# Rings as single buffers taken in turn, tiles taken by their first writer, and a new written-out order, in a fused linear attention and channel-mix kernel

## The chip, the cores and the metric

The kernel runs on one core of a Trainium2 chip. Its time is device microseconds of one launch. The profile's span is the stretch in which the profiler saw work on the core.

## The reference

Two layers follow each other. The first is linear attention with a learned feature map (8 batches, 8 heads, 576 positions, head size 64, 128 features):

```
phi(x) = concat(exp(p), exp(-p)),  p = x @ w_phi - max|x @ w_phi|
kv  = einsum('bhsf,bhsd->bhfd', phi(k), v);   z = sum over s of phi(k)
out = (phi(q) @ kv) / (phi(q) . z + 1e-6)
```

The heads are then laid side by side (x: 8 x 576 x 512), and the second layer mixes channels:

```
x_prev = x shifted by one position (zero ahead)
xk = mu_k*x + (1-mu_k)*x_prev;   xr = mu_r*x + (1-mu_r)*x_prev
k  = max(xk @ w_k, 0)            # 512 -> 1024
v  = (k*k) @ w_v                 # 1024 -> 512
out = sigmoid(xr @ w_r) * v
```

Inputs and output are float32; matmuls run on bfloat16.

## The kernel before

**Units of work.** Attention goes by pairs of heads, numbered n = 4b + a (batch b from 0 to 7, pair a from 0 to 3), so 32 pairs. The channel mix goes by batch b, in blocks of 512 positions, and once per two batches for the 64 positions that are left over of each ("edge"). Every step of a unit has a short name, and these names are used throughout:

- Loads of batch b: `lk`, `lq` (k and q, issued by POOL's software queue, L321, into tile nat), `lv` (v, issued by SP or POOL, L327, into vt). For batches 2 to 7, `tr b.0` and `tr b.2` (L352) transpose the first and second half of nat into qkT by DMA, issued by SP. For batches 0 and 1, PE does it (`pt`, L338), and `pa`, `pb` copy the result. The first batches' loads are split finer (`lk0.1`, `lk0.2`). `wk`, `wr`, `wv` load the weights.
- Pair n: `kp`, `qp` project k and q on PE (L566); `rk`, `rq` take the maximum of |.| on DVE (L579, L584); `em` (ACT, L591), `mh` (DVE or POOL), `mt` (PE) and `mc` (DVE or ACT) prepare the scale; `ea` is the exponential of k on ACT (L605); `va`, `vb` multiply v by the scale, on POOL or DVE (L597); `qt` projects q again, transposed (L630, L636); `qa`, `qb` are its exponentials on ACT (L643; `eb` is the second exponential of k); `kv` (L656, L662) is the product of phi(k) and v, `kc` its copy; `nd` (L677) gives numerator and denominator, `ra` the reciprocal (DVE, L685), `rd` the division into x_sc (DVE, L689).
- Pair n, then: x has to be transposed into xs. Below n = 8 PE does it (`xt`, L715, with copies `xe`, `xf`); from n = 8 on SP issues a DMA transpose (`xz`, L700) and `xu` does two small copies. `df` is the difference of neighbouring positions (L726), `xa` and `xb` the two mixes (DVE, L732).
- Edge of attention, per batch: the left-over rows of all pairs go through `tp` (PE, L466), `rt`, `mhe`, `mte`, `mce`, `eme`, `ekt`, `qte`, `eqe`.
- Channel mix of batch b: `h b.0` to `h b.7` (PE, L810), `rl` (relu, ACT L206 or DVE L208), `sq` (square, ACT L212, or DVE or POOL L214), `r b.0` to `r b.3` (PE, L829), `th` (tanh form of the sigmoid, ACT, L835), `v b.0` to `v b.3` (PE, L843, eight matmuls each), `ob` (DVE, L849) and `so` (the store, two DMAs on SP, L856). Edges `he`, `rle`, `sqe`, `re`, `the`, `ve`, `obe`, `soe` are the same for the left-over positions.

**What sets the order.** The string ORDER at the head of the file lists all steps, and Plan.order() turns it into the list in which they are emitted. Scheduling by the framework is off. Each engine, and SP as a queue, runs its own steps strictly in the order of this list; waits between engines come from which tiles a step reads and writes. In a word such as `kp5:0`, the number behind the colon is the PSUM place; `/POOL` names the engine where there is a choice; `+2@1` adds two filler matmuls. Words that end in `.d` mark where a DMA's end stood in the list and emit nothing.

**Buffers.** A tile in SBUF is asked for from a pool with a number of buffers, `bufs`, and the pool gives out one that is free. BUFS lists the numbers: nat 2, qkT 2, vt 3, k and q exponentials 2 each, kk 2, krelu 3, rt 3, ob 4, x 3, d (diff) 2 and so on. The tile of a relu (krelu) is asked for in `h`, ahead of the matmuls that fill PSUM, that of a gate (rt) in `r`, and that of an output (ob) in `v`:

```
s["kr", fc] = mm.tile([128, 512], BF, name="krelu", bufs=BUFS["krelu"])   # in h
s["t", ci] = mm.tile([128, DM], BF, name="rt", bufs=BUFS["rt"])           # in r
s["o", ci] = mm.tile([128, DM], FP, name="ob", bufs=BUFS["ob"])           # in v
```

Work overlaps across batches: while the channel mix of batch b runs on PE, the attention of batch b + 1 and the loads of batch b + 2 and later go on.

Of the kernel before, what the change touches and what calls it, by code (L numbers as in the profile page):

```python
# [31 lines left out]
eb3 pt6.1:0 pt7.0:1 va2/POOL pb6/DVE tr6 qt2:2 pa7/ACT ra1 rd1 mte0.2:0 qa2 lk2.0 lk2.0.d pt7.1:1
mce0.2/DVE qp5:0 pb7/DVE tr7 qte0.2:0 lq2.0 lq2.0.d qb2 rq5 tp1.0:1 xt0:1 va3/POOL eqe0.2 kv2:2
rt1.0 xf0/ACT xe0/ACT kp4:0 mh4/POOL mt3:0 kc2/ACT rk4 xt1:1 df0/POOL mc3/ACT ekt1.0 nd2:2 ra2 ea4
vb3/POOL xe1/DVE qt3:1+1@0 rd2 mt4:0 xf1/ACT mc4/ACT df1/DVE qa3 xt2:1 xa0 kv3:2 eb4 mhe1.0/DVE
xe2/DVE mte1.0:0+1@0 xb0 kc3/ACT kp5:0 qb3 qt4:2 xa1 eme1.0 xf2/DVE nd3:1 rk5 mce1.0/ACT df2/POOL
qa4 ra3 qb4 rd3 lv1.2/POOL lv1.2.d ea5 xa2 xt3:0+7@1 qp6:2 xb1 qte1.0:1 xe3/ACT qp7:1 eb5 xf3/DVE
df3/DVE xa3 em4 qt5:0+1@0 eqe1.0 rq6 vb4/POOL h0.0:0 qa5 va4/POOL rq7 kp6:2 qb5 h0.1:1 rk6 mh6/POOL
kp7:1 rl0.1/ACT kv4:0 va5/POOL rl0.0/ACT tr2.0 tr2.0.d tr8 tr9 mt6:1 kc4/DVE ea6 h0.2:0 rk7 vb5/POOL
eb6 xb2 kv5:0+1@2 mc6/ACT sq0.0/ACT xb3 nd4:2 tr2.2 tr2.2.d tr10 tr11 em6 ea7 h0.3:1 kc5/DVE  # L40
vb6/POOL ra4 rd4 nd5:0 eb7 vb7/POOL rl0.3/DVE qt6:2 rl0.2/ACT ra5 qp8:1 rd5 qa6 lv2.0/SP lv2.0.d
sq0.1/POOL r0.0:1 rq8 qb6 va6/POOL qp9:0 h0.4:0 rq9 th0.0 sq0.3/POOL sq0.2/ACT qt7:2 kv6:1 rl0.4/DVE
qa7 lk3.0 lk3.0.d tp2.0:0 kc6/DVE h0.5:1 mh8/POOL rt2.0 qb7 va7/POOL xt4:0 rl0.5/ACT kp8:1 xf4/DVE
# [12 lines left out]
eqe3.0 r1.0:1 rq12 em12 r1.1:0 th1.0 va12/POOL ea13 so0.0 so0.0.d rq13 qp14:1 h1.2:1 vb12/POOL eb13
xz10 xz10.d rq14 nd11:2 rl1.2/ACT va13/POOL qp15:0 th1.1 ra11 lv3.2/SP lv3.2.d h1.3:1 rd11 xu8/ACT
xu9/POOL sq1.1/ACT so0.3 so0.3.d mh12/POOL rq15 kv12:1 sq1.2/ACT vb13/POOL kp14:2 kc12/ACT h1.4:0
rk14 rl1.3/ACT mh14/POOL sq1.3/POOL mt12:1 kv13:1 mc12/ACT so0.1 so0.1.d rl1.4/DVE ea14 kp15:0
# [101 lines left out]
def kernel(  # L161
# [141 lines left out]
    def get(dct, key, pool, shape, dtype, name, **kw):  # L303
        if key not in dct:
            dct[key] = pool.tile(shape, dtype, name=name, **kw)
# [711 lines left out]
```

## Time and profile before

| | |
|---|---|
| time, median of 3 runs | 277.98 us (277.68 to 287.12) |
| span of the profiled execution | 275.3 us (no other time of that execution is given) |
| granted TensorE clock | 1.00 in each window of 10 us |
| PE, DVE, ACT, POOL busy | 261.7, 234.6, 223.1, 142.4 us |
| read from and written to HBM | 33.62 and 9.44 MB |
| instructions | 8865 |

The page gives the busy time of each engine, then the span in 40 slices of 6.9 us (a digit is the busy share in tenths), the DMA queues, the chain of work that ended last, the costliest groups of instructions (operation, tiles, shape, number | busy time, mean ns of one | idle time ahead of them and what ended it), and the DMA issues with the time to landing. "SPq" is SP's queue of issues. Matmuls of PE are pipelined, and their ends are modelled, so a busy PE isn't one at its peak.

### The profile page before, as it was taken

Reading aid. Unit: us, or ns where it says so; the run is one execution under the profiler, and the core shown is the slowest. Engines: PE = TensorE matmul, PEld = TensorE weight load, DVE = VectorE, ACT = ScalarE, POOL = GpSimd, SP = SyncE. Lnnn points to the kernel's source line nnn. Section 1 sums busy time; section 2 is a strip of 40 time slices with the busy share of each in tenths; the row PEclk is TensorE's granted clock in tenths of the full one; section 3 lists DMA queues with packets and bytes.
Section 4 is the critical chain, followed back from the end, with each engine's and each line's share of the span. In section 5 each row is a group of like instructions: output and inputs, shape, how many; then the busy total and the mean of one; then the engine's idle time right before and its main releaser. Section 6 shows DMA issues by size and latency. Waiting matters only on the chain.

```text
span 275.3 us, 8865 instructions
## 1 busy us (share of the span) xinstructions
PE 261.7 (95%) x3682; PEld 154.1 (56%) x3730; DVE 234.6 (85%) x388; ACT 223.1 (81%) x413; POOL 142.4 (52%) x193
## 2 busy tenths in 40 slices
PE   7899889999899999999999999999999999999993
PEld 3567656566555566555565666555566565444542
DVE  6999999999799989999999889998889897864222
ACT  3899999999899997899898999789987777616330
POOL 5799557976818682633459465821931611300200
PEclk9999999999999999999999999999999999999999
DMA  7999999599999899759699998981725324142134
GB/s 147 285 209 250 209 213 174 114 235 175 238 129 200 202 219 185 155 127 248 99 166 164 215 249 142 171 255 41 161 89 88 77 52 100 42 110 67 29 88 116
DMA packets 65817, 42.89 MB, mean 156 GB/s; under 512 B 47152, under 2 KB 57008, under 8 KB 65776
## 3 DMA queue, kind: packets, MB, share of 16 engines
q1 hardware_dynamic: 54496, 27.54, 49.3%
q0 software_dynamic: 11056, 14.42, 29.1%
q8 instruction: 29, 0.48, 0.8%
q10 hardware_dynamic: 224, 0.36, 0.5%
q14 instruction: 12, 0.10, 0.1%
HBM read 33.62 MB, written 9.44 MB: 156 GB/s over the span
## 4 chain that ended last, share of the span: by engine, by line
PE 75%; DVE 8%; ACT 6%; issue 4%; DMA 3%; POOL 2%; SPq 0%; POOLq 0%; ACTq 0%
PE ps_h L810 19%; PE ps_v L843 17%; PE ps_r L829 9%; PE ps_nd L677 5%; PE ps_kv L656 5%; DMA qkT<-nat 3%; PE ps_he L897 3%; PE ps_ve L929 3%; PE ps_k L566 2%; PE ps_qT L630 2%; PE ps_q L566 2%; PE ps_qT L636 2%; ACT k L605 2%; DVE nmk L579 2%; PE ps_f L292 1%
## 5 line engine op out<-in xcount | busy, mean ns | idle before, releaser
L597 POOL TENSOR_TENSOR v<-vt,v 128x576 bf16<-128x576 f32 x59 | 69.8, 1203 | 33.5 <-ACT v L591 31.1
L605 ACT ACTIVATE k<-ps_k 128x1024 bf16<-128x1024 f32 x64 | 64.8, 1047 | 1.3 <-DVE nmk L579 1.3
L643 ACT ACTIVATE q<-ps_qT 128x1024 bf16<-128x1024 f32 x64 | 63.8, 1054 | 1.8 <-PE ps_qT L636 1.7
L810 PE MATMUL ps_h<-xk,wk_bf 128*128 128x512 bf16 x235 | 60.5, 380 | 1.2
L843 PE MATMUL ps_v<-wv_bf,kk 128*128 128x512 bf16 x244 | 58.2, 379 | 0.6
L579 DVE TENSOR_REDUCE nmk<-ps_k 128x8 f32<-128x1024 f32 x32 | 38.8, 1217 | 1.8 <-PE ps_k L566 1.5
L584 DVE TENSOR_REDUCE nmq<-ps_q 128x8 f32<-128x1024 f32 x32 | 38.3, 1217 | 1.6 <-PE ps_q L566 1.4
L843 PEld LDWEIGHTS <-kk 128*128 128x128 bf16 x256 | 24.1, 98 | 27.3
L810 PEld LDWEIGHTS <-wk_bf 128*128 128x128 bf16 x256 | 22.7, 97 | 25.0 <-issue 0.7
L206 ACT ACTIVATE krelu<-ps_h 128x512 bf16<-128x512 f32 x48 | 28.8, 611 | 9.3 <-PE ps_h L810 9.3
L726 POOL TENSOR_TENSOR diff<-xs 128x576 bf16<-128x576 bf16 x15 | 20.2, 1346 | 28.8 <-ACT xs L706 12.7
L214 POOL TENSOR_TENSOR kk<-krelu 128x512 bf16<-128x512 bf16 x18 | 19.1, 1068 | 30.3 <-ACT krelu L206 26.6
L849 DVE SCALAR_TENSOR_TENSOR ob<-rt,ps_v 128x512 f32<-128x512 bf16 x32 | 21.7, 682 | 14.3 <-PE ps_v L843 12.7
L829 PE MATMUL ps_r<-wr_bf,xr 128*128 128x512 bf16 x116 | 31.1, 380 | 0.7
L835 ACT ACTIVATE rt<-ps_r 128x512 bf16<-128x512 f32 x32 | 19.7, 615 | 8.8 <-PE ps_r L829 8.7
L732 DVE SCALAR_TENSOR_TENSOR xk<-diff,mu_k_t,xs 128x576 bf16<-128x576 bf16 x32 | 26.7, 839 | 0.1
L689 DVE TENSOR_TENSOR x_sc<-ps_nd,rden 128x640 bf16<-128x640 f32 x32 | 26.0, 817 | 0.6
L732 DVE SCALAR_TENSOR_TENSOR xr<-diff,mu_r_t,xs 128x576 bf16<-128x576 bf16 x32 | 25.6, 806 | 0.1
L656 PE MATMUL ps_kv<-v,k 64*128 64x65 bf16 x1024 | 22.4, 190 | 0.5 <-ACT q L643 0.2
L566 PEld LDWEIGHTS <-qkT 64*128 64x128 bf16 x512 | 16.5, 94 | 11.0 <-issue 8.0
L656 PEld LDWEIGHTS <-k 64*128 64x128 bf16 x1024 | 19.3, 94 | 5.7 <-issue 1.8
L677 PE MATMUL ps_nd<-kv,q 128*128 128x65 bf16 x512 | 21.4, 193 | 0.0
(102 smaller groups left out, 414.3 us busy)
## 6 DMA issues: line engine op xcount, KB each, us to landing
out_dram<-ob SPq DMA_DIRECT2D x70, 128.0 KB, 2.5
vt<-in_v_dram SPq DMA_DIRECT2D x11, 576.0 KB, 6.1
nat<-in_k_dram POOLq DMA_DIRECT2D x6, 576.0 KB, 7.8
nat<-in_q_dram POOLq DMA_DIRECT2D x6, 576.0 KB, 8.0
vt<-in_v_dram POOLq DMA_DIRECT2D x4, 576.0 KB, 6.0
wk_bf<-in_moe_w_k_dram POOLq DMA_DIRECT2D x2, 512.0 KB, 11.4
wv_bf<-in_moe_w_v_dram POOLq DMA_DIRECT2D x2, 512.0 KB, 10.6
nat<-in_k_dram POOLq DMA_DIRECT2D x3, 288.0 KB, 6.9
```

Source lines behind the costliest of these rows:

```text
L206: nc.scalar.activation(out_, in_, AF.Relu, scale=HALF)
L579: nc.vector.tensor_reduce(t[:, j, :], s["k"].rearrange("p a (g f) -> p (a g) f", f=128), axis=AX.X, op=ALU.max, apply_absolute_value=True, ...
L584: nc.vector.tensor_reduce(t[:, j, :], s["q"].rearrange("p a (g f) -> p (a g) f", f=128), axis=AX.X, op=ALU.max, apply_absolute_value=True, ...
L597: (nc.vector if eng == "DVE" else nc.gpsimd).tensor_tensor(vb[:, a, pn, :, 0:64], vt[b, a // 2][:, a % 2, :].rearrange("p (s d) -> p s d", ...
L605: nc.scalar.activation(s[f"k{pn}"], s["k"].rearrange("p a (g f) -> p (a g) f", f=128), AF.Exp, scale=(1.0 if pn == 0 else -1.0))
L643: nc.scalar.activation(t.rearrange("f x (a p) -> f x a p", a=2), s["qT"].rearrange("f a (x p) -> f x a p", p=64), AF.Exp, scale=(1.0 if pn ...
L656: nc.tensor.matmul(ps[:, hh, pn * 65:(pn + 1) * 65], lhsT=s[f"k{pn}"][r, c, :], rhs=vb[r, a, pn, 2 * g + par, :], start=(pn == 0 and c == ...
L677: nc.tensor.matmul(ps[:, bk, o * 65:(o + 1) * 65], lhsT=tail if sl < 2 else s[f"q{pn}"][:, 2 * G + h, :], rhs=s["kv"][:, h, pn, :], start= ...
L732: nc.vector.scalar_tensor_tensor(out=t[:, a, (b % 2) * S:(b % 2 + 1) * S], in0=s["d"], scalar=mu[:, a:a + 1], in1=xs[:, a, 0:S], op0=ALU.m ...
L810: nc.tensor.matmul(ps, lhsT=wk_bf[:, c, fc * 128:(fc + 1) * 128], rhs=xkt[bp][:, c, m0:m0 + 512], start=(c == 0), stop=(c == NDC - 1))
L829: nc.tensor.matmul(ps, lhsT=xrt[bp][:, c, m0 + ci * 128:m0 + (ci + 1) * 128], rhs=wr_bf[:, c, :], start=(c == 0), stop=(c == NDC - 1))
L843: nc.tensor.matmul(ps, lhsT=s["kk"][:, fc, ci * 128:(ci + 1) * 128], rhs=wv_bf[:, fc, :], start=(fc == 0), stop=(fc == NFC - 1))
```

## The change

Three things change, and nothing that is computed.

1. Every ring of buffers becomes a set of tiles with one buffer each, named by their place (`krelu.0`, `krelu.1`, ...), which are taken in turn by a counter. BUFS gets entries for rden (3, what the pool gave it before) and kke (1).
2. The tiles krelu, rt and ob are asked for by the step that first writes them (`rl`, `th`, `ob`) and no longer by the matmuls ahead of it.
3. ORDER is written anew: the same steps with other places in the list, and for some another engine (the square `sq`, the relu `rl`, the small copies `mc`, `xu`, `kc`, the difference `df`, a v multiply and the v loads). PSUM places change with it. The diff shows only two stretches of the list, where batches 4 and 5 are fetched.

```diff
+    used = {}
+
+    def slot(kind):
+        i = used[kind] = used.get(kind, -1) + 1
+        return i % BUFS[kind]
+
+    def ring(pool, kind, shape, dtype, name, i=None):
+
+        i = slot(kind) if i is None else i
+        return pool.tile(shape, dtype, name=name, tag=f"{name}.{i}", bufs=1)
+
     nat, qkT, vt = {}, {}, {}
 
-    def get(dct, key, pool, shape, dtype, name, **kw):
+    def get(dct, key, pool, kind, shape, dtype, name):
         if key not in dct:
-            dct[key] = pool.tile(shape, dtype, name=name, **kw)
+            dct[key] = ring(pool, kind, shape, dtype, name)
         return dct[key]
...
-                s["kr", fc] = mm.tile([128, 512], BF, name="krelu", bufs=BUFS["krelu"])
                 if fc == 0:
-                    s["kk"] = mm.tile([128, NFC, 512], BF, name="kk")
+                    s["kk"] = ring(mm, "kk", [128, NFC, 512], BF, "kk")
...
         def rl(fc):
             def f(eng):
+                s["kr", fc] = ring(mm, "krelu", [128, 512], BF, "krelu")
                 relu(eng, s["kr", fc], s[fc])
             return f
...
             def f():
+                s["t", ci] = ring(mm, "rt", [128, DM], BF, "rt")
                 nc.scalar.activation(s["t", ci], s["r", ci], AF.Tanh, scale=0.5)
...
             def f():
+                s["o", ci] = ring(mm, "ob", [128, DM], FP, "ob")
                 nc.vector.scalar_tensor_tensor(out=s["o", ci], in0=s["t", ci], scalar=1.0,
...
-mce3.0/DVE ob0.3 tr4.0 tr4.0.d tr16 tr17 h1.0:0 qa11 xb6 h1.1:1 qb11 ra10 xb7 kv11:2 rl1.0/ACT rd10
-kp13:0 eme3.0 tr4.2 tr4.2.d tr18 tr19 sq1.0/POOL qte3.0:0 kc11/DVE rl1.1/ACT qp12:1 rk13 qp13:2
...
-ra14 rd13 df11/POOL qb15 rd14 re0:1 xu12/POOL so1.1 so1.1.d sqe0.1/DVE ob1.2 kp17:2 the0 kv15:0 rk17
-xz13 xz13.d qt16:1 kc15/ACT v1.3:1 xb11 ea17 tr5.2 tr5.2.d tr22 tr23 sqe0.0/DVE eb17 xa10 nd15:0
...
+r1.0:1 rk13 r1.1:0 xz8 tr4.2 so0.2 xz9 lv3.2/SP xz10 so0.1 tr4.0 xz8.d sq1.0/ACT lv3.0.d xz9.d th1.0
...
+xz11.d xu11/DVE ra13 rd13 df11/POOL tr5.0 xz12 so1.1 lv4.0/SP so1.0 xz13 tr5.2 xz13.d xz12.d so0.2.d
...
```

The order of SP's queue around these places, before: ... so0.2, xz8, xz9, tr4.0, tr4.2, so0.0, xz10, lv3.2, so0.3, so0.1, lv4.0, xz11, so1.0, xz12, tr5.0, so1.1, xz13, tr5.2, ...; after: ... xz8, tr4.2, so0.2, xz9, lv3.2, xz10, so0.1, tr4.0, so0.0, lv4.2, so0.3, xz11, tr5.0, xz12, so1.1, lv4.0, so1.0, xz13, tr5.2, ...

## The prediction

> **What bounds the kernel now.** I read the page's engine table and slices first, then the table of 10 us windows, then the chain that ended last, the waits, and the timeline of SP, whose queue the new order rearranges most.
>
> ```profile
> PE 261.7 (95%) x3682; PEld 154.1 (56%) x3730; DVE 234.6 (85%) x388; ACT 223.1 (81%) x413; POOL 142.4 (52%) x193
> PE   7899889999899999999999999999999999999993
> PE 75%; DVE 8%; ACT 6%; issue 4%; DMA 3%; POOL 2%; SPq 0%; POOLq 0%; ACTq 0%
> ```
>
> TensorE is busy nearly throughout; the digits below 9 all lie in the first eleven slices (75 us), but for the last one. The windows (start:end, then busy us of PE, PEld, DVE, ACT, POOL) say what holds it there:
>
> ```profile
> 30.00:40.00 10.00, 8.38 (x138) 5.38 (x139) 9.78 (x21) 10.00 (x21) 3.93 (x5) 1.00 1.16 227
> 70.00:80.00 10.00, 8.82 (x144) 5.43 (x143) 8.66 (x16) 8.92 (x14) 4.67 (x6) 1.00 1.10 208
> 110.00:120.00 10.00, 9.95 (x131) 5.58 (x133) 9.42 (x14) 8.76 (x17) 5.55 (x5) 1.00 0.81 163
> 250.00:260.00 10.00, 9.95 (x59) 4.99 (x58) 3.24 (x7) 5.37 (x9) 2.04 (x2) 1.00 0.05 10
> ```
>
> Up to about 70 us DVE and ACT are full and PE has gaps; from 80 us on PE has 9.8 of 10 or more in every window I read. The last real stall of PE is this (timeline of PE; in brackets its idle time and what ended it):
>
> ```profile
> 71.63 0.29 PE L466 MATMUL ps_e<-wph,qkT 64*128 64x128 bf16 x4 [1.07 <-DMA qkT<-nat]
> ```
>
> So there are two rules. Before about 75 us a gain must come from DVE and ACT, or from loads that they wait for. After it PE can't be gained on by order, and any new wait of PE is paid one to one. I also summed PE's stream by its own spacings (0.86 us for each four-matmul h or r, 1.73 for a v, and so on): 241.8 us of nominal work, so 275.3 - 241.8 = 33.5 us outside it. About 6 of these are head and tail; of the other 27.5, 19.3 lie before 80 us and 8 after. Those 8 are what the 33 passages into 64-row matmuls and back cost (8/33 = 0.24 us each), and order decides their number.
>
> **The change, part by part.**
>
> *Rings of single buffers, and krelu, rt and ob taken by their writer.* No instruction is added. In the old order most rings are already taken in turn (kk, nat, qkT, k, q, kv, x_sc, nmk, mT, rt), and the exceptions (diff, krelu, ob, nmq, mTe) have no long wait of their own in the list of waits; the long ones there name producers (`ob <- PE ps_v` 12.7 us, `krelu <- PE ps_h` 9.3 us), not a buffer's reader. Value 0; bounds -0.5 and +0.5 us, half of that 1.07 us stall either way, as nothing is shown nearer.
>
> *New order, PE.* The same 3730 matmuls and 33 fills. Passages fall from 66 to 65 (half-passages, both ways), and the PE work ahead of h1.0 is 58.6 us in both orders: 0, with ±0.3 for a passage.
>
> *New order, who computes.* Squares: POOL 18 to 22, ACT 24 to 28, DVE 22 to 14. Relus: ACT 48 to 44, DVE 16 to 20. Copies: mc seven from ACT to DVE, xu six from ACT and POOL to DVE, kc one to ACT. Two more diff (df) and one v multiply on POOL, two more v loads issued there. At 420 ns a square on DVE, 641 on ACT, 1068 on POOL, 611 and 679 ns a relu on ACT and DVE, 285 and 218 a small copy, 474 and 1346 ns a diff, the engines go DVE -1.7, ACT 0, POOL +9.5 us (by start-to-start spacing). POOL is at 52%, so its 9.5 us are hidden unless one of them stands ahead of a v multiply that kv needs.
>
> [...] The rows have a square of 512 columns at 1068 ns on POOL against 420 on DVE, 2.5 times. [...] No term of the sum uses this.
>
> *Head (to 75 us).* Added up along the order, DVE's work ahead of the points that PE waits for falls by 1.0 us (k's maximum of pair 9), 0.7 (pairs 10, 11) and 0.5 (the mix of pair 7, which opens h1.0, ended at 78.1 with 0.3 us to spare); ACT's ahead of the exponentials grows by 0.5 to 2. Loads of batch 2 are issued some 4 us earlier. I take -0.6; bounds -2 (also the 1.07 us stall and the pair-9 gain whole) and +1.5 (ACT's 2 less the 0.5).
>
> *SP's queue: the main term.* Each batch's q and k get transposed by DMA in two halves (tr b.0 and tr b.2). In the old order the halves stand side by side; in the new one stores (so), x transposes (xz) and v loads (lv) stand between them, and SP issues strictly in order.
>
> ```profile
> 78.84 6.50 SPq L352 DMA_TRANSPOSE qkT<-nat  x2
> 105.61 3.16 SPq L352 DMA_TRANSPOSE qkT<-nat  x1
> 112.55 2.78 SPq L352 DMA_TRANSPOSE qkT<-nat  x1
> 92.50 0.54 SPq L327 DMA_DIRECT2D vt<-in_v_dram  x1
> 93.15 1.43 SPq L700 DMA_TRANSPOSE xs<-x_sc  x1
> ```
>
> (Timeline of SP: start, time on the queue.) From these: a tr occupies SP 2.4 to 3.4 us, an xz 1.2, a pair of store halves 1.2, a v load 0.55. Landing after issue:
>
> ```profile
> qkT<-nat SPq DMA_TRANSPOSE x12, 6.0
> vt<-in_v_dram SPq DMA_DIRECT2D x11, 576.0 KB, 6.1
> xs<-x_sc SPq DMA_TRANSPOSE x24, 3.2
> DMA to landing us min/median/max: 4.6/6.0/7.9
> ```
>
> (Median us in the DMA view; the last line is the tile view of qkT.) I walked the new queue by hand with these:
> - Batch 4. tr4.2 goes first (77), then so, xz9, lv3.2, xz10, so, and tr4.0 at 85.9 where it was 78.85. Landing 4.6 to 6.5 later, 90.5 to 92.4; PE wants qp16 at about 91.7. 0 to 0.8 us; I take 0.3.
> - Batch 5. tr5.0 still waits for its load (105.5), issue to 108.7; then xz12 110, so 111.2, lv4.0 111.8, so 113, xz13 114.4, tr5.2 114.5. It lands at 119.1 to 122.4 (4.6 to 7.9). Before, it landed at 117.2 and the work that takes it (tp5.0) ran at 122.9; the new order moves tp5.0 up to about 118.5. Wait of PE 0.6 to 3.9; with the median 6.0 it is 2.0, and I take 1.8, since tp5.0 can follow its own first half a little. At the same place lv4.0, issued at 89.4 before, now goes at 111.8; it lands at 116.0 to 122.4 (the vt tile's 4.2 to 10.6), and three v multiplies of 1.2 us on POOL follow before kv16, wanted at 118.8: 0.8 to 7.2 us at the same instruction chain, so not added to the other but the larger of both.
> - Batch 6: tr6.0 issued near 140.6, some 5 us later than before, lands 145.2 to 148.5, wanted at 144.9 and later by what PE has already lost: 0 to 1.5, I take 0.3. Batch 7: lands before it is wanted.
>
> *ACT in the tail.* ACT's work ahead of some exponentials of q grows (pair 17 +4.0 us, 21 +3.2, 25 +2.0); at pair 25 the old order had no slack. ACT is idle for 10.4 us between 80 and 190 us of the old trace, mostly waiting for h and r, which can take this: 0; bounds 0 and +2.
>
> **Sum.** 275.3 - 0.6 + 0.3 + 1.8 + 0.3 = 277.1 us of span. The median shown is 277.98, that is 2.7 above the span; the same 2.7 gives 279.8 us, +1.8 or 0.6%. The page gives no time of the profiled execution but its span.
>
> [...] The rows agree in landing only (6.0 against 6.1 us for these two); on the queue a tr holds SP for 2.4 us or more against 0.54 for a v load. If a tr cost SP 0.54 us, the batch 5 wait would shrink by the 3.16 - 0.54 = 2.6 us and vanish, and the sum would be 278.0.
>
> **Rivals.**
> - *Everything arrives in time.* Landings at 4.6 us and early POOL: the waits above are 0 to 0.6, and the head's gain stands: 275.3 - 0.6 + 0.3 + 2.7 = 277.7. For it: the windows from 80 us on show no PE wait on DMA, and slacks of 6 to 7 us before. Against it: these slacks are what the new queue spends.
> - *The transposes and v loads become the bound between 85 and 150 us* (slower by over 2%). One mechanism: SP's queue is in order, so each load set behind a store or x transpose inherits that one's wait for DVE; place batches 4 to 6, L352 and L327. At the late ends: 0.8 + 7.2 + 1.5 + 2 (ACT, whose work queues up behind) - 0.6 = +10.9, or 288.9 us; I call it 285, the near half of what lies past the bound. It decides once the sum of waits passes 5.6 us, that is once lv4.0 takes over 9 us to land. For it: the list of SP's waits has 30.0 us of xz behind x_sc; an xz of the old order (93.15) landed 8.9 us after issue, right behind a v load. Against it: a typical v load needs 6.3.
> - *The head shrinks* (faster by over 2%): it takes 5.6 of the 19.3 us lost before 80 us. For it: loads of batch 2 and the weights move. Against it: DVE and ACT are at 9.7 to 10 there and lose only 0.5 to 1 us of work. 272.0 us.
> - *The change does nothing by its rings, and the order only shuffles covered work*: 278.0; falls in with the first.
>
> **Chances and range.** Forecast 0.44 (278.3 to 283.0), all in time or nothing 0.20 (276.5 to 278.3), transposes as bound 0.26 (283.5 to 289), head shrinks 0.10 (270 to 272.4). Faster by over 2%: 0.10; slower: 0.26; within 2% (about what a measurement of this kernel can tell from no change): 0.64. The range takes in the forecast, the first rival and the near half of the slower one; 274.5 to 287 leaves out 0.09 below and 0.08 above.
>
> **What would show it.** Right: new PE waits of 1 to 3 us on `DMA qkT` or on `v L597` around 118 to 122 us, nearly nothing else after 80 us, h1.0 reached some 0.6 us sooner, POOL's busy time up by 9 us, eight fewer squares on DVE. Wrong: no PE wait after 80 us (first rival); several such waits at batches 4, 5 and 6, or waits on ACT's q behind them (second); h1.0 before 74 us (third). The forecast falls too if the new order's PE waits stem from a PSUM place still being read, which I have not priced apart from these.

## The result, and the profile after

The changed kernel takes 305.62 us (median of 4 runs, 302.5 to 307.66), the kernel before 280.51 us; the ratio is 1.087 with a 95% interval of 1.075 to 1.098. Run once more beside other kernels it took 301.31 us (298.37 to 304.01), ratio 1.063 (1.046 to 1.080). So it is slower by 6 to 9%, where the forecast was 279.8 us and the range ended at 287.0. Some runs of both kernels are disturbed and longer (those of the kernel before spread from 276.8 to 291.1 us; the undisturbed ones of the changed kernel took 302.5 and 303.8), and the ratios leave the disturbed ones out. The profiled execution of the changed kernel took 302.5 us, with a span of 300.7 us.

The page of the changed kernel: engines, PE by slices, the granted clock by slices, and the shares of the chain that ended last.

```profile
PE 269.3 (90%) x3684; PEld 157.9 (52%) x3730; DVE 241.9 (80%) x395; ACT 223.6 (74%) x400; POOL 150.3 (50%) x201
PE   6879787599789979979999599999999999999994
PEclk9979999989959999998999799999999999999999
PE 63%; DMA 10%; DVE 10%; ACT 7%; issue 3%; SPq 2%; POOL 2%; DVEq 0%; ACTq 0%; POOLq 0%
```

PE now has holes after 75 us too, and its clock, which was 1.00 throughout, falls to 0.5 for a while in five places, four times for 3.41 us and once for 6.83. In the chain, DMA goes from 3 to 10%. The holes are few and short; here they are in the timeline of PE (in brackets the idle time and what ended it):

```profile
17.62 0.22 PE L499 MATMUL ps_me<-ident,mhlt 128*128 128x128 bf16 x1 [2.08 <-DVE qkT L202]
59.99 0.61 PE L646 MATMUL ps_qT<-qkT,wph 64*128 64x512 bf16 x2 [3.50 <-DVE nmq L598]
83.31 0.40 PE L480 MATMUL ps_e<-wph,qkT 64*128 64x128 bf16 x4 [2.33 <-DVE x_sc L707]
108.18 0.40 PE L580 MATMUL ps_q<-wph,qkT 64*128 64x128 bf16 x8 [0.98 <-DMA qkT<-nat]
133.78 0.37 PE L518 MATMUL ps_qe<-qkT,wph 64*128 64x512 bf16 x1 [1.78 <-DVE ob L956]
168.81 1.03 PE L580 MATMUL ps_q<-wph,qkT 64*128 64x128 bf16 x16 [3.37 <-DMA qkT<-nat]
```

In the first three and in the fifth PE has its data and waits for a place in PSUM that DVE has yet to read: the result of `pt` at 17.62, of `qp` at 59.99, of `nd` at 83.31, of `ve` at 133.78. The other two wait for a DMA transpose of q and k.

What each is worth is seen by comparing when PE reaches the same step in both traces (start of its first weight load). The lag grows to 25.8 us; the two spans differ by 25.4:

| PE reaches | before | after | lag | grows by | between, in the changed kernel |
|---|---|---|---|---|---|
| qp3 | 15.6 | 19.4 | 3.7 | 3.7 | wait that ends at 17.62 |
| h0.4 | 49.7 | 54.6 | 4.9 | 1.2 | two short waits at 45 to 47 us |
| v0.0 | 63.0 | 73.4 | 10.4 | 5.5 | wait that ends at 59.99 |
| h1.0 | 78.4 | 93.3 | 15.0 | 4.6 | waits that end at 83.31 and 84.30 |
| v1.0 | 97.5 | 114.5 | 17.0 | 2.0 | wait that ends at 108.18 |
| v2.0 | 128.5 | 149.3 | 20.8 | 3.8 | wait that ends at 133.78 |
| h4.0 | 170.8 | 195.9 | 25.1 | 4.4 | wait that ends at 168.81 |
| ve3.1 (last) | 269.9 | 295.7 | 25.8 | 0.6 | |

The six holes above are 14.0 us together. PE's idle time grew by 17.8 us in all, and its busy time, at the lower clock, by 7.6. Not all of the first row is waiting: ahead of qp3 the new order has PE do 13 more weight loads (for qte0 and qt1).

Behind the first three stands DVE. Its timeline in the changed kernel (start, time, line, tiles), with POOL's for two of the places below:

```profile
14.80 1.15 DVE L631 CAST mhl<-nmq 128x8 bf16<-128x8 f32 x1
15.99 1.18 DVE L632 TENSOR_TENSOR mhl<-nmq,mhl 128x8 bf16<-128x8 f32 x1
...
43.59 1.70 DVE L752 SCALAR_TENSOR_TENSOR xk<-diff,mu_k_t,xs 128x576 bf16<-128x576 bf16 x1
...
54.08 4.72 DVE L611 TENSOR_TENSOR v<-vt,v 128x576 bf16<-128x576 f32 x1
...
79.15 3.28 DVE L752 SCALAR_TENSOR_TENSOR xk<-diff,mu_k_t,xs 128x576 bf16<-128x576 bf16 x1
```

```profile
43.52 3.93 POOL L611 TENSOR_TENSOR v<-vt,v 128x576 bf16<-128x576 f32 x3 [2.50 <-ACT v L605]
...
53.96 0.78 POOL L339 DMA_DIRECT2D vt<-in_v_dram  x1
54.76 3.42 POOL L611 TENSOR_TENSOR v<-vt,v 128x576 bf16<-128x576 f32 x3
58.12 0.79 POOL L333 DMA_DIRECT2D nat<-in_k_dram  x1
```

The same instructions take 0.165, 0.174, 0.81, 0.75 and 0.81 us elsewhere, so the five are 9.3 us longer, more than the whole rise of DVE's busy time (7.3). vb6 (L611) begins on DVE at 54.08 and ends at 58.80, that is 0.6 us after POOL's third multiply has ended. The mix at 43.59 is different: it ended 0.6 us after the first of POOL's three multiplies, and the second one took longer in its turn (1.68 us instead of 1.2). All of them read SBUF only; DVE's instructions that read PSUM at such times keep their length (the `rk` at 47.48, beside POOL's v multiplies, took 1.21 us, and the mean of all 32 is 1.22). The kernel's own tables mark exactly these steps (mh, v multiplies, df, xa, xb, sq) with `port=True`, a mark that I had passed over.

### The profile page after: what moved, and what is told of

It is laid out like the page before. It is cut to its first block, busy times and chain, and to the rows that moved or that the text cites. A ratio compares the mean times of both kernels' runs of the same rounds, so it can differ in the third digit from the quotient of the medians.

```text
span 300.7 us, 8845 instructions
## 1 busy us (share of the span) xinstructions
PE 269.3 (90%) x3684; PEld 157.9 (52%) x3730; DVE 241.9 (80%) x395; ACT 223.6 (74%) x400; POOL 150.3 (50%) x201
## 4 chain that ended last, share of the span: by engine, by line
PE 63%; DMA 10%; DVE 10%; ACT 7%; issue 3%; SPq 2%; POOL 2%; DVEq 0%; ACTq 0%; POOLq 0%
PE ps_v L862 16%; PE ps_h L829 14%; PE ps_r L848 8%; DMA qkT<-nat 6%; PE ps_nd L695 5%; PE ps_kv L674 4%; DVE nmq L598 3%; ACT k L621 3%; PE ps_qT L646 3%; DMA out_dram<-ob 3%; PE ps_he L917 2%; PE ps_q L580 2%; PE ps_qT L652 2%; DVE nmk L593 2%; PE ps_ve L948 2%
## 5 line engine op out<-in xcount | busy, mean ns | idle before, releaser
L611 POOL TENSOR_TENSOR v<-vt,v 128x576 bf16<-128x576 f32 x60 | 69.7, 1184 | 38.3 <-ACT v L605 29.6
L621 ACT ACTIVATE k<-ps_k 128x1024 bf16<-128x1024 f32 x64 | 65.5, 1040 | 2.2 <-DVE nmk L593 2.1
L829 PE MATMUL ps_h<-xk,wk_bf 128*128 128x512 bf16 x236 | 62.5, 388 | 2.5 <-DVE xk L752 1.0
L214 POOL TENSOR_TENSOR kk<-krelu 128x512 bf16<-128x512 bf16 x22 | 22.8, 1040 | 36.1 <-ACT krelu L206 31.7
L746 POOL TENSOR_TENSOR diff<-xs 128x576 bf16<-128x576 bf16 x17 | 22.8, 1341 | 31.4 <-DVE xr L752 12.3
L829 PEld LDWEIGHTS <-wk_bf 128*128 128x128 bf16 x256 | 23.3, 99 | 27.0 <-issue 3.8
L206 ACT ACTIVATE krelu<-ps_h 128x512 bf16<-128x512 f32 x44 | 26.5, 602 | 11.3 <-PE ps_h L829 11.2
L848 PE MATMUL ps_r<-wr_bf,xr 128*128 128x512 bf16 x117 | 32.3, 386 | 0.8 <-issue 0.2
L752 DVE SCALAR_TENSOR_TENSOR xk<-diff,mu_k_t,xs 128x576 bf16<-128x576 bf16 x32 | 29.0, 913 | 0.1
L580 PEld LDWEIGHTS <-qkT 64*128 64x128 bf16 x512 | 17.7, 97 | 20.7 <-issue 14.0
L674 PE MATMUL ps_kv<-v,k 64*128 64x65 bf16 x1024 | 23.4, 194 | 0.9 <-DVE nmk L593 0.5
L674 PEld LDWEIGHTS <-k 64*128 64x128 bf16 x1024 | 20.4, 97 | 5.2 <-issue 4.2
```

The lines of the kernel that those rows point to most:

```text
L206: nc.scalar.activation(out_, in_, AF.Relu, scale=HALF)
L611: (nc.vector if eng == "DVE" else nc.gpsimd).tensor_tensor(vb[:, a, pn, :, 0:64], vt[b, a // 2][:, a % 2, :].rearrange("p (s d) -> p s d", ...
L621: nc.scalar.activation(s[f"k{pn}"], s["k"].rearrange("p a (g f) -> p (a g) f", f=128), AF.Exp, scale=(1.0 if pn == 0 else -1.0))
L674: nc.tensor.matmul(ps[:, hh, pn * 65:(pn + 1) * 65], lhsT=s[f"k{pn}"][r, c, :], rhs=vb[r, a, pn, 2 * g + par, :], start=(pn == 0 and c == ...
L752: nc.vector.scalar_tensor_tensor(out=t[:, a, (b % 2) * S:(b % 2 + 1) * S], in0=s["d"], scalar=mu[:, a:a + 1], in1=xs[:, a, 0:S], op0=ALU.m ...
L829: nc.tensor.matmul(ps, lhsT=wk_bf[:, c, fc * 128:(fc + 1) * 128], rhs=xkt[bp][:, c, m0:m0 + 512], start=(c == 0), stop=(c == NDC - 1))
```

## The experiments

All but the probes start from the changed kernel or the kernel before and change words of ORDER; the order of a word in the list is its place on its engine.

**The rings and the order apart.** e1_rings is the changed code with the old ORDER, e2_order the old code with the new ORDER.

> The changed kernel's code (rings of single buffers in turn, krelu, rt and ob taken by their first writer) with the old ORDER. Theory A (the order alone costs the time, the rings nothing): 278 to 281 us, within 1% of before. Rival B (the rings tie each tile to one place, and the waits for it cost time in any order): at least 8 us more than before, 288 or above.

> The old code (pools that give out a buffer, krelu, rt and ob asked for by the matmul) with the new ORDER. Theory A: 302 to 308 us, as the changed kernel. Rival B: 290 us or less, since the pool may give out another buffer than the one in turn, above all where the edge output waits 2.1 us for a store at 131 us.

Measured: e1_rings 277.9 us, ratio to before 0.999 (0.995 to 1.003); e2_order 299.35 us (298.76 to 301.68), ratio 1.080 (1.070 to 1.090). The loss comes with the order; the rings by themselves cost nothing. (e2_order lies between the two figures that were expected, 302 to 308 and 290 or less.) One difference between e2_order and the changed kernel goes back to the rings. In the changed kernel the edge output waits on DVE for a store:

```profile
133.04 0.69 DVE L956 SCALAR_TENSOR_TENSOR ob<-rt,ps_ve 128x512 f32<-128x512 bf16 x1 [2.12 <-DMA out_dram<-ob]
```

With four places taken in turn, obe0 gets the place of ob1.0, whose store so1.0 the new order issues after tr5.0, xz12, so1.1 and lv4.0. In e2_order this wait isn't there, and PE's lag at the end is 23.0 us against 25.8; by the medians (299.4 against 301.3 and 305.6, spread over 5 us) the difference isn't resolved.

**vb6 on POOL.** e3_vb6:

```diff
-qp8:0 h0.4:0 r0.0:1 qa6 qb6 sq0.3/ACT th0.0 vb6/DVE rq8 rq9 lv2.2/POOL va6/POOL va7/POOL vb7/POOL
+qp8:0 h0.4:0 r0.0:1 qa6 qb6 sq0.3/ACT th0.0 vb6/POOL rq8 rq9 lv2.2/POOL va6/POOL va7/POOL vb7/POOL
```

> The changed kernel with one word changed: the v multiply vb6 on POOL instead of DVE. In the changed kernel this multiply took 4.72 us on DVE (0.75 us elsewhere), while POOL issued a load and ran three v multiplies one behind the other; then PE stood still for 3.5 us and its clock went to 0.5. Theory L (DVE's instructions that read two tiles from SBUF can't run while POOL works without a break): the stall at 56 to 60 us goes, with its slow clock, 4 to 6 us less than the changed kernel, 297 to 300. Rival (PE would have waited there anyway, for the next thing in line): less than 1.5 us gained.

Measured: 300.19 us (299.91 to 301.76). The windows of 10 us (PE, PEld, DVE, ACT, POOL busy, granted clock, DMA share, GB/s), first the changed kernel, then e3_vb6:

```profile
50.00:60.00 10.00, 6.13 (x117) 3.92 (x118) 9.82 (x12) 7.17 (x12) 7.66 (x8) 0.97 0.37 112
60.00:70.00 10.00, 9.70 (x165) 6.27 (x168) 9.13 (x12) 8.55 (x17) 4.95 (x8) 0.86 0.87 145
```

```profile
50.00:60.00 10.00, 9.51 (x181) 5.82 (x181) 8.84 (x13) 9.97 (x16) 7.05 (x7) 1.00 0.38 115
60.00:70.00 10.00, 7.20 (x125) 4.29 (x126) 10.00 (x13) 8.55 (x18) 8.23 (x15) 1.00 0.95 149
```

PE's timeline of e3_vb6:

```profile
69.41 0.29 PE L695 MATMUL ps_nd<-kv,tq 128*128 128x65 bf16 x4 [2.40 <-DVE nmq L598]
```

The hole that ends at 59.99 us is gone, so DVE's delay made it. But 10 us later there is one of 2.40 us: there the square sq0.5 on DVE met POOL and took 2.81 us for 0.42. Mending one meeting moved the next. Of the 4 to 6 us that were expected 2.4 came, by PE's lag at the end (23.4 us against 25.8).

**All three meetings ahead of PE.** e4_locks adds:

```diff
-pt3.1:1 mh1/DVE pa3/DVE mte0.1:0+1@3 pb3/DVE lq1.0.d lk1.2.d lq1.2.d tr2 tr3 mce0.1/DVE qp2:1 mt1:1
+pt3.1:1 mh1/POOL pa3/DVE mte0.1:0+1@3 pb3/DVE lq1.0.d lk1.2.d lq1.2.d tr2 tr3 mce0.1/DVE qp2:1 mt1:1
...
-lk4.0.d em10 ea11 qa9 qb9 eb11 mc10/DVE ob0.1 ra8 xa5 rd8 va10/POOL lq4.0 v0.2:1 ob0.2 vb10/POOL
+lk4.0.d em10 ea11 qa9 qb9 eb11 mc10/DVE ob0.1 ra8 rd8 xa5 va10/POOL lq4.0 v0.2:1 ob0.2 vb10/POOL
```

> As e3_vb6, and the other two places where DVE stood behind POOL ahead of PE: mh1 on POOL instead of DVE (its two instructions took 2.3 us on DVE at 15 us, 0.34 elsewhere), and the mix xa5 set behind the division rd8 instead of ahead of it (the mix took 3.28 us at 79 us, 0.81 elsewhere). Theory L: the head's 3.8 us and part of the stall at 81 us go as well, 7 to 11 us less than the changed kernel, 292 to 297; what is left is the DMA side. Rival: no more than e3_vb6 gains.

Measured: 296.74 us (293.09 to 297.75). PE reaches h1.0 with a lag of 8.0 us instead of 15.0. At v2.0 the gain is down to 4.3 us (16.5 against 20.8): PE, now earlier, waits longer for the same store, 3.92 us at 129 us. At the end the lag is 21.0 us.

**SP's queue.** e7_sp moves three words of the changed kernel; e5_all does this on top of e4_locks, with sq0.5 on ACT and xu10 behind vb13.

```diff
-r1.0:1 rk13 r1.1:0 xz8 tr4.2 so0.2 xz9 lv3.2/SP xz10 so0.1 tr4.0 xz8.d sq1.0/ACT lv3.0.d xz9.d th1.0
+r1.0:1 rk13 r1.1:0 xz8 tr4.0 tr4.2 so0.2 xz9 lv3.2/SP xz10 so0.1 xz8.d sq1.0/ACT lv3.0.d xz9.d th1.0
...
-xz11.d xu11/DVE ra13 rd13 df11/POOL tr5.0 xz12 so1.1 lv4.0/SP so1.0 xz13 tr5.2 xz13.d xz12.d so0.2.d
+xz11.d xu11/DVE ra13 rd13 df11/POOL so1.0 tr5.0 xz12 so1.1 lv4.0/SP xz13 tr5.2 xz13.d xz12.d so0.2.d
...
-tr6.2 soe0 so1.3.d v2.2:1 xa14 ra17 ob2.1 rd17 mt20:0 ob2.2 qp22:1 qp23:2 qt19:0 mc20/ACT qa19 qb19
+tr6.0 tr6.2 soe0 so1.3.d v2.2:1 xa14 ra17 ob2.1 rd17 mt20:0 ob2.2 qp22:1 qp23:2 qt19:0 mc20/ACT qa19 qb19
...
-kv19:2 kp21:0 h3.1:1 eqe5.0 ea20 rl3.1/ACT so2.0 xz16 xz16.d xu16/POOL tr6.0 xz17 so2.1 mh22/DVE
+kv19:2 kp21:0 h3.1:1 eqe5.0 ea20 rl3.1/ACT so2.0 xz16 xz16.d xu16/POOL xz17 so2.1 mh22/DVE
```

> The changed kernel with SP's order alone mended as in e5_all (tr4, tr6 halves side by side, so1.0 ahead of tr5.0). Theory: the stalls at 107 (1.0), 132 (1.8) and 166 us (3.4) go with the slow clock of the last two: 7 to 10 us less than the changed kernel. Rival (the in-order queue isn't the cause, transfers are late by contention): less than 3 us gained.

> e4_locks, and the square sq0.5 on ACT instead of DVE (it took 2.8 us on DVE in e4_locks, 0.42 elsewhere), and the queue of SP mended in three places: tr4.0 and tr4.2 side by side, tr6.0 and tr6.2 side by side with the first half first, the store so1.0 ahead of tr5.0; xu10 behind vb13 on POOL. Theory (DVE behind POOL, SP's order, and the slow clock after each stall of PE make the whole loss): the stalls of 2.4, 3.9, 1.0 and 2.8 us of e4_locks at 62, 125, 101 and 160 us go with their slow clock, 281 to 287 us. Rival (something else of the order costs most): 291 or more.

Measured: e7_sp 305.89 us (304.61 to 307.16), no gain (PE's lag at the end is 27.9 us against 25.8); e5_all 299.0 us (297.54 to 300.53), not better than e4_locks. Both were expected to gain and didn't. The waits that were aimed at did go (108, 133 and 168 us), and others came in their place (in e5_all also one of 2.97 us at 77.46, on the transpose of batch 3). The timelines of e5_all, POOL and then PE at the first place:

```profile
100.67 0.23 POOL L202 COPY xs<-xs 128x63 bf16<-128x63 bf16 x1 [3.56 <-DMA xs<-x_sc]
```

```profile
104.46 0.29 PE L636 MATMUL ps_m<-ident,mhl 128*128 128x128 bf16 x1 [3.21 <-POOL mhl L632]
```

And DVE and then PE at the second:

```profile
166.89 1.29 DVE L202 COPY xs<-xs 128x63 bf16<-128x63 bf16 x1 [3.45 <-DMA xs<-x_sc]
```

```profile
169.37 0.61 PE L480 MATMUL ps_e<-wph,qkT 64*128 64x128 bf16 x8 [3.62 <-DVE nmq L598]
```

Two transposes ahead of an xz delay that xz; its small copies xu stand in line on POOL or DVE, and a whole engine waits for a 0.2 us copy, with mh or rq behind it that PE needs. The new order puts six of the xu copies more on DVE. So neither of these two rearrangements found room in this queue: what was moved forward took its time from what it passed.

**One store, and a mend without touching the queue otherwise.** e11_so swaps so1.0 and so1.1; e12_mend is e4_locks with this swap, sq0.5 on ACT, and lk3.0, lq3.0 ahead of lv2.2. e10_again is the changed kernel beside them. e11_so against the changed kernel, and below it the lines of e12_mend that e4_locks and e11_so don't have:

```diff
-xz11.d xu11/DVE ra13 rd13 df11/POOL tr5.0 xz12 so1.1 lv4.0/SP so1.0 xz13 tr5.2 xz13.d xz12.d so0.2.d
+xz11.d xu11/DVE ra13 rd13 df11/POOL tr5.0 xz12 so1.0 lv4.0/SP so1.1 xz13 tr5.2 xz13.d xz12.d so0.2.d
```

```diff
-qp8:0 h0.4:0 r0.0:1 qa6 qb6 sq0.3/ACT th0.0 vb6/POOL rq8 rq9 lv2.2/POOL va6/POOL va7/POOL vb7/POOL
-rl0.4/DVE lv2.0.d qt7:0 kv6:2 tp2.0:1 rt2.0 qa7 kc6/ACT xt4:1 xe4/DVE xf4/DVE lk3.0 lq3.0 lk3.0.d
+qp8:0 h0.4:0 r0.0:1 qa6 qb6 sq0.3/ACT th0.0 vb6/POOL rq8 rq9 lk3.0 lq3.0 lv2.2/POOL va6/POOL va7/POOL vb7/POOL
+rl0.4/DVE lv2.0.d qt7:0 kv6:2 tp2.0:1 rt2.0 qa7 kc6/ACT xt4:1 xe4/DVE xf4/DVE lk3.0.d
...
-th0.2 mc8/ACT xa4 sq0.5/DVE rq11 vb8/POOL va8/POOL nd6:2 mte2.0:1 h0.7:0 ra6 mce2.0/DVE rd6 nd7:0
+th0.2 mc8/ACT xa4 sq0.5/ACT rq11 vb8/POOL va8/POOL nd6:2 mte2.0:1 h0.7:0 ra6 mce2.0/DVE rd6 nd7:0
```

> The changed kernel once more, beside the others on the same chip: 302 to 308 us by every theory; it is what e11_so and e12_mend are compared with.

> The changed kernel with two words swapped: the stores so1.0 and so1.1, so that the store that frees the buffer of the edge output goes out first, one store and a v load earlier. Theory R (in-turn rings make the edge output of batches 0 and 1 wait for just this store, which the order puts last): the wait of 2.1 us on DVE for the store and PE's stall of 1.8 us at 132 us go with their slow clock, 2 to 5 us less than e10_again. Rival (PE waits there for the next thing anyway): within 1 us.

> e4_locks with sq0.5 on ACT, the stores so1.0 and so1.1 swapped, and POOL's loads lk3.0 and lq3.0 issued ahead of lv2.2 and three v multiplies, as early as in the old order. The queue of SP is otherwise left alone. Theory (waits of SP's queue pass on to the in-order engines when it is moved, so only causes that stand alone can be mended): the stalls of e4_locks at 62 (2.4) and 125 us (3.9) go, the one of 3.0 us at 77 us of e5_all doesn't come, those at 101 (1.0) and 160 us (2.8) stay: 285 to 291 us. Rival (each mended wait is followed by another of the same size): 294 or more.

Measured: e10_again 301.31 us (298.37 to 304.01), a little under what was expected; e11_so 300.5 us (299.53 to 302.41); e12_mend 294.87 us (291.14 to 299.38). In e11_so the edge output runs without the wait:

```profile
131.31 0.69 DVE L956 SCALAR_TENSOR_TENSOR ob<-rt,ps_ve 128x512 f32<-128x512 bf16 x1
```

and from v1.0 to v2.0 the lag grows by 0.3 us instead of 3.8 (2.8 in e10_again); at the end it is 23.3 us against 25.8 and 25.9. In the medians the gain is 0.8 us, less than the spread, so by time it isn't shown. e12_mend is the best form of the new order that I found, its lag 18.4 us, and still 4.3% above before (ratio 1.043, 1.027 to 1.060); it ends up at the rival's 294 or more, with one wait on qkT of 3.94 us at 160 us and one of 2.25 us at 78 us. Of the head's 15.0 us at h1.0 it still has 7.0, in eight waits of 0.5 to 2.3 us that weren't followed up one by one. No kernel beat the one before beyond its interval.

**The slow clock.** In the changed kernel's trace each hole of 1.78 us and more comes with a stretch at a clock of 0.5 (from 18.37, 59.33, 83.22, 134.42 and 168.55 us on, 3.41 us long, the third 6.83); the mean of the run is 0.966. e6_fill puts 14 filler matmuls each ahead of qt7 and qp24, into two of the holes:

```diff
-rl0.4/DVE lv2.0.d qt7:0 kv6:2 tp2.0:1 rt2.0 qa7 kc6/ACT xt4:1 xe4/DVE xf4/DVE lk3.0 lq3.0 lk3.0.d
+rl0.4/DVE lv2.0.d qt7:0+14@1 kv6:2 tp2.0:1 rt2.0 qa7 kc6/ACT xt4:1 xe4/DVE xf4/DVE lk3.0 lq3.0 lk3.0.d
...
-lv6.0/POOL v2.3:1 eb20 sq3.0/ACT ea21 em20 eb21 rd18 xb14 h3.3:0 ob2.3 qp24:2 qp25:1 qt20:0 rq24
+lv6.0/POOL v2.3:1 eb20 sq3.0/ACT ea21 em20 eb21 rd18 xb14 h3.3:0 ob2.3 qp24:2+14@1 qp25:1 qt20:0 rq24
```

> The changed kernel with 14 filler matmuls (3 us at full clock) put ahead of qt7 and of qp24 each, where PE stood still for 3.5 and 3.4 us and then had a clock of 0.5 for about 4.4 us. They take away no wait. Theory C (the stall itself lowers the clock, and that doubles the price): no slow clock behind these two, 3 to 4.5 us less than the changed kernel. Rival (the clock falls for another reason, or what follows is held up by DVE anyway): no change, or slower by the fillers that outlast the wait.

Measured: 300.89 us (299.23 to 302.96), against 305.62 and 301.31 of the changed kernel, so not resolved by time. The windows, the changed kernel first, then e6_fill:

```profile
160.00:170.00 10.00, 6.47 (x73) 3.70 (x69) 5.96 (x12) 6.12 (x11) 4.50 (x6) 0.93 0.79 152
170.00:180.00 10.00, 9.73 (x142) 6.04 (x142) 8.78 (x16) 7.62 (x13) 7.26 (x9) 0.90 0.97 230
```

```profile
160.00:170.00 10.00, 9.54 (x87) 4.90 (x84) 6.19 (x12) 6.21 (x12) 4.84 (x6) 1.00 0.81 173
170.00:180.00 10.00, 9.19 (x164) 5.96 (x165) 8.85 (x17) 7.94 (x13) 7.63 (x10) 1.00 0.97 210
```

The clock stays at 1.00, so the hole is what lowers it. But little is won: from h0.4 to v0.0 the lag grows by 4.8 us instead of 5.5 (5.2 in e10_again), from v2.0 to h4.0 by 4.0 instead of 4.4 (4.6). Part of the gain the fillers took back, since they outlasted both waits: rq8 was done at 60.14 us and qt7 began at 60.57, tr6.0 had landed at 167.90 and qp24 began at 168.64. With these 0.4 and 0.7 us added, a slow stretch cost about 0.8 to 1.3 us here (an estimate from the two places), where half speed for 3.41 us could cost 1.7 and 1.5 to 2.25 were expected for each. Why it is less isn't shown; it may be that PE, at full speed, would have waited for engines that are as late as it is.

**What holds DVE, by itself.** e8_probe, e9_probe and e13_probe add chains on POOL and single instructions on DVE behind the kernel before (they leave nothing out). The core of e8_probe, first the cases for DVE, then the gaps for PE:

```diff
+            for _ in range(n):
...
+                    nc.gpsimd.tensor_tensor(pG, pT, pA, op=ALU.mult)
+            nc.vector.tensor_tensor(pD, pT, pps, op=ALU.mult)
+            dve()
...
+            nc.vector.tensor_tensor(pD, pT, pB, op=ALU.mult)
...
+            for i in range(45):
+                nc.tensor.matmul(t, lhsT=(pL if i == 0 else ones)[:, 0:128], rhs=ones, start=True, stop=True)
+            for i, w in enumerate(gap):
+                if i == 0:
+                    nc.scalar.copy(pL[:, 0:w], t[:, 0:w])
```

e9_probe and e13_probe add cases with the v multiply of the kernel (576 columns, one input broadcast) in place of the plain one and with loads issued by POOL around the chain; e9_probe has the gaps in another order, and in e13_probe POOL's multiplies write places of their own.

> The kernel before, with work added behind its own, so its total time says nothing. Part one: POOL runs 0, 1, 2, 4, 8 multiplies of 512 columns one behind the other while DVE runs one multiply of two SBUF tiles, a copy of one SBUF tile, or a multiply with one tile in PSUM. Theory L: DVE's two-input multiply ends with the last of POOL's, about n times 1.07 us, and the one with PSUM is not held (0.7 us). Rival (only POOL's software DMA issue holds DVE): 0.4 us in all cases. Part two: 45 matmuls, then an idle time of PE set by a chain of ACT copies of about 0.4 to 3.5 us, twice over. Theory C: the clock stays at 1.0 behind gaps up to about 1.1 us, and is at 0.5 for 3 to 5 us behind gaps of 1.8 us and more. Rival: it falls only behind the gaps over 3 us.

> The kernel before, with work added behind its own, so its total time says nothing. The earlier probe held DVE's two-input multiply only to the end of POOL's first instruction. Here POOL runs chains of the kernel's own v multiply (float32 in, a broadcast column, steps of 65), of plain multiplies, and a load issued ahead of and behind three v multiplies, while DVE runs a plain multiply of two SBUF tiles, a v multiply or a mix. Theory L2 (POOL's v multiplies keep the port from one to the next): DVE's instruction ends with the last of a chain of v multiplies, 1.2, 2.3, 3.5, 4.7 us for one to four, and after one instruction (under 1.6 us) with plain multiplies. Rival (it needs the load issued on POOL ahead of them): under 1.6 us for all chains without a load, over 3 us with it. Part two: 20 gaps of PE of 1.4, 1.8, 2.0 and 2.7 us in mixed order behind 40 to 52 matmuls. [...] Rival (only the length counts, from 2.1 us on): none of the 2.0 us gaps.

> The kernel before, with work added behind its own, so its total time says nothing. In the second probe each of POOL's instructions wrote the same tile, and there were 0.08 us between one and the next; DVE's two-input instruction got in there (0.8 to 1.2 us). In the changed kernel POOL's v multiplies write different tiles, and the next starts 0.05 us before the last ends. Here they write different tiles. Theory L3 (DVE's instruction with two SBUF inputs waits until POOL leaves a gap): it ends with the last of the chain: about 3 us behind three multiplies, 4 behind four, 6 behind six; the one with an input in PSUM takes 0.7. Rival L4 (only with a load issued on POOL ahead of the chain): under 1.2 us for the chains without a load, over 3 us for those with one. Rival L5 (neither; it is the place of the data): under 1.2 us in all.

Measured, on DVE, beside POOL's chains: a multiply of two SBUF tiles takes 0.42 us alone and 0.75 beside 1, 2, 4 or 8 plain multiplies (e8_probe); 0.46 alone and 0.80 beside 1 to 4 v multiplies (e9_probe); 0.93 beside three independent ones (e13_probe); a copy of one SBUF tile takes 0.62 to 0.78 beside them and 0.29 alone (e8_probe, e13_probe); a multiply with one input in PSUM keeps its 0.69. From the timeline of DVE in e13_probe (the multiply of two SBUF tiles alone, then beside three v multiplies; a multiply with one input in PSUM beside three):

```profile
291.18 0.46 DVE L1032 TENSOR_TENSOR xs<-wr_bf,v 128x576 bf16<-128x576 bf16 x1
...
293.68 0.93 DVE L1032 TENSOR_TENSOR xs<-wr_bf,v 128x576 bf16<-128x576 bf16 x1
...
317.93 0.69 DVE L1044 TENSOR_TENSOR xs<-v,ps_p 128x512 bf16<-128x512 bf16 x1
```

In each probe DVE got in at POOL's first change from one instruction to the next, after waiting for the rest of the running one. L2 and L3 fall, and of L the part holds that an instruction waits while POOL's runs, and that PSUM frees it. L4 wasn't put to the test: in e13_probe DVE ran ahead of the load in those cases, and in e9_probe's one such case (0.27 us between load and chain) DVE got in at the first change.

The kernel's own traces speak for L4, though no run varied this alone. In the eleven traces of the new order, a DVE instruction with inputs in SBUF waited past a change from one v multiply to the next 21 times, and each time POOL had issued a load 0.02 us ahead of the first multiply (as at 54.08 and 79.15). The mix at 43.59 has no load within 2.5 us ahead of POOL's multiplies, and in all eleven traces it got in at the first change. The issue of a load alone didn't hold DVE: a mix that began at 114.18, as POOL began to issue one, took 0.76 us.

Part two, PE's gaps, is told in the last section. In e8_probe theory C missed: gaps of 1.82 and 2.03 us left the clock at 1.0 there. In e9_probe the gaps of 2.03 us lowered it twice and once not, those of 1.82 us never.

Two more runs looked at it in the kernel. e14_gap issues lk3.0 behind va6 and lq3.0 behind va7, with vb6 still on DVE. e15_lock is e1_rings with mh1 on DVE.

```diff
-qp8:0 h0.4:0 r0.0:1 qa6 qb6 sq0.3/ACT th0.0 vb6/DVE rq8 rq9 lv2.2/POOL va6/POOL va7/POOL vb7/POOL
-rl0.4/DVE lv2.0.d qt7:0 kv6:2 tp2.0:1 rt2.0 qa7 kc6/ACT xt4:1 xe4/DVE xf4/DVE lk3.0 lq3.0 lk3.0.d
+qp8:0 h0.4:0 r0.0:1 qa6 qb6 sq0.3/ACT th0.0 vb6/DVE rq8 rq9 lv2.2/POOL va6/POOL lk3.0 va7/POOL lq3.0 vb7/POOL
+rl0.4/DVE lv2.0.d qt7:0 kv6:2 tp2.0:1 rt2.0 qa7 kc6/ACT xt4:1 xe4/DVE xf4/DVE lk3.0.d
```

```diff
-mhe0.1/DVE mh1/POOL pa2/DVE pb2/DVE tr2 eb1 vb0/POOL pt3.0:1+2@3 pt3.1:0 pa3/DVE qb0 pb3/DVE tr3
+mhe0.1/DVE mh1/DVE pa2/DVE pb2/DVE tr2 eb1 vb0/POOL pt3.0:1+2@3 pt3.1:0 pa3/DVE qb0 pb3/DVE tr3
```

> The changed kernel with the loads lk3.0 and lq3.0 issued between POOL's three v multiplies (va6, va7, vb7) instead of behind them; vb6 stays on DVE. Theory L (DVE gets the port while POOL issues a load): vb6 ends during the first of these issues, at most 3 us after its start instead of 4.72, and PE's stall of 3.5 us ahead of qt7 shrinks by 1.5 to 2.5 us. Rival (DVE is held until the last multiply, whatever lies between): vb6 takes 6 us, the stall is longer than 3.5.

> The old order in the changed kernel's code (as e1_rings) with one word changed: mh1 on DVE instead of POOL, as the new order has it, so that DVE's two small instructions meet POOL's two v multiplies at 14 to 16 us. Theory L: they take 1 to 2.3 us together instead of 0.34, PE waits 1 to 2.5 us more there, and the time is 1 to 4 us above e1_rings: 279 to 282. Rival (the loss needs the rest of the new order): as e1_rings, 277.5 to 278.5.

Measured: in e14_gap (296.0 us, one run) vb6 takes 2.99 us instead of 4.72, and PE's wait there is 1.77 us instead of 3.50 (timelines of DVE, then PE):

```profile
52.21 2.99 DVE L611 TENSOR_TENSOR v<-vt,v 128x576 bf16<-128x576 f32 x1
```

```profile
56.39 0.39 PE L646 MATMUL ps_qT<-qkT,wph 64*128 64x512 bf16 x2 [1.77 <-DVE nmq L598]
```

POOL's issue of lk3.0 ran from 54.01 to 54.80, and vb6 ended at 55.20: here DVE got in after one multiply instead of three, and the rival falls. But a load between two multiplies doesn't always let DVE in: the first instruction of mh1 waited across one in five other traces of the new order (2.80 us in e10_again, from 14.78, with the load at 15.54). PE's lag grows by 4.0 us from h0.4 to v0.0 instead of 5.5. In e15_lock (279.38 us, 277.3 to 281.82, ratio 1.002, 0.991 to 1.013) the two small instructions took 0.16 and 0.17 us: on DVE they were done at 13.9 us, as POOL's chain began. The meeting that the run was to bring about didn't happen, so it only says that mh1 on DVE costs nothing by itself.

## Why the prediction was wrong

- *Rings and first writers, 0 ± 0.5:* right with the old order (0.999). With the new one the turn of the ob ring makes obe0 wait 2.1 us and PE 1.78; I had looked at long waits in the old order only, where the store comes in time.
- *PE's passages, 0:* nothing speaks against it; after the last hole, from h4.0 to the end, the lag grows by 0.6 us.
- *Who computes (DVE -1.7, POOL +9.5, hidden):* this step failed first. POOL's busy time did rise, by 7.9 us, and DVE's squares did fall. But DVE's busy time rose by 7.3 us. I took each duration from a row of the old order, in which POOL's and DVE's SBUF-only work seldom meet: there the longest of DVE's mixes took 1.49 us. In the new order they meet, and the instructions shown above are 9.3 us longer for it; the durations belonged to the order, not to the instruction. mh1, which moved to DVE, was not in my list of what moves, and the list's net count (one v multiply more on POOL) hid that vb6 went the other way.
- *Head, -0.6, bounds -2 and +1.5:* measured +15.0 at h1.0. The mechanism above is about half of it: e4_locks takes 7.0 us away, e12_mend 8.0. What makes the other 7.0 us stays open. The bounds came from the same rows, so they could not hold it.
- *SP's queue, 0.3 + 1.8 + 0.3:* the mechanism (a queue strictly in order, loads behind stores and x transposes) was right, the sizes weren't. Batch 4 waited 0.98 us at qp16, a little above the 0.8 of the late end. In batch 5 tr5.2 landed at 136.48 us and PE took it at 139.1, no wait; instead so1.0, two places earlier in the same queue, held obe0 and then PE for 1.78 us; the wait for lv4.0 (0.8 to 7.2) didn't come. Batch 6 waited 3.37 us at qp24, where I had 0.3 and at most 1.5: tr6.0 was issued at 164.06, behind a pair of store halves that held SP for 2.35 us instead of 1.2 and an x transpose, and took 4.7 us (the median of these transposes is 5.3):

```profile
160.31 2.35 SPq L876 DMA_DIRECT2D out_dram<-ob  x2
162.70 1.31 SPq L720 DMA_TRANSPOSE xs<-x_sc  x1
164.06 2.75 SPq L364 DMA_TRANSPOSE qkT<-nat  x1
```

- *ACT in the tail, 0:* right, no long wait of PE after 85 us is on ACT.
- *The slower rival* named the queue and got the sign; its price (+10.9 at the late ends) is near what the lag grew by from h1.0 to h4.0: 2.0 + 3.8 + 4.4 = 10.2 us. That is luck in good part: 7.2 of the 10.9 were for lv4.0 and 2 for ACT, which cost nothing, while the ob store and batch 6 cost more than was reckoned for them. The other 15.0 us, in the head, were in none of the cases.
- *No gain:* what the new order was to give, earlier loads of batch 2 and less work on DVE, went under in the first wait at 17 us.
- *The sign that was named last:* waits for a PSUM place still being read, which the forecast had not priced apart. Four of the six holes, 9.7 of their 14.0 us, are such waits.

What would have shown it ahead: the old trace has 64 mixes between 0.75 and 1.49 us. Its three longest diffs and mixes (0.85, 1.09 and 1.49 us) each stood beside a POOL instruction. The longest, on DVE and then POOL:

```profile
237.74 1.49 DVE L732 SCALAR_TENSOR_TENSOR xk<-diff,mu_k_t,xs 128x576 bf16<-128x576 bf16 x1
...
237.57 1.04 POOL L214 TENSOR_TENSOR kk<-krelu 128x512 bf16<-128x512 bf16 x1 [6.08 <-ACT krelu L206]
```

Whoever had looked there had the meeting and its price, 1.49 us for a mix of 0.81, though only beside one POOL instruction and not a chain, and `port=True` in the code said where to look.

## What to carry to other kernels

Durations from a profile hold for the neighbours that an instruction had there (here 0.75 us became 4.72): before pricing a new order by them, look in the old trace for the few instances that were longer than their group and see what ran beside them. In an order by hand, an instruction that can be late (a store's buffer, a small copy behind a DMA) holds everything behind it on its engine or queue (in e5_all a copy of an xu kept DVE idle for 3.45 us), so a mend that moves it ahead of others is to be priced by what it passes; here moving three words of SP's queue (e7_sp, e5_all) gained nothing. And where PE has hardly any idle time, a few holes count: six of 1 to 3.5 us are 14.0 of the 25.4 us between the two spans.

## What the runs showed of the hardware

- DVE instructions with inputs in SBUF alone waited while POOL's instruction ran: 0.75 us became 2.99 (e14_gap) or 4.72 and 0.81 became 3.28 (changed kernel), 0.42 became 2.81 (e3_vb6); one with an input in PSUM took 0.69 us with and without it (e8_probe, e13_probe). In probes the wait ended with POOL's running instruction, in the kernel it lasted over up to three. Whenever it outlasted a change between two v multiplies, a load had been issued on POOL directly ahead of them; whether that is the cause wasn't tested.
- PE's clock. In the probes (e8_probe, e9_probe), none of 25 gaps of up to 1.82 us (from the modelled end of one matmul to the start of the next) lowered it; at 2.03 us it fell in 2 of 5 cases, from 2.3 us on in all 4, and then 8 or 9 matmuls of 512 columns took 0.43 us each, 3.4 to 3.8 us together. In the changed kernel a gap of 1.78 us did it too, in e2_order one of 1.63, while gaps of 2.33 (e14_gap), 2.37 (e10_again) and 2.54 us (e3_vb6) didn't. So the length alone doesn't decide; what else does wasn't tested. In the changed kernel's trace all changes of the clock lie a whole number of 3.41 us apart, and in the kernels every slow stretch behind a hole lasted 3.41 or 6.83 us.
- Two transposes of qkT issued beside a load on POOL (tr3.0 and tr3.2 at 67.2 and 70.4 us, lk4.0 at 67.3) took 12.9 and 13.9 us to land, and the second held SP for 9.73 us; in the kernel before no tr took over 7.9. In e12_mend they took 12.7 and 12.3 us, again beside lk4.0; in e10_again, the same kernel as the changed one, 9.7 and 5.6. This wasn't tested further.
